# Two loads cut by partitions into 120 and 8: cosformer attention and a leaky-ReLU FFN on one core

## The chip, the core and the metric

The kernel runs on one core of a Trainium2 chip. The core has five engines with a queue of instructions each: TensorE (PE in the profile; its weight loads are PEld), VectorE (DVE), ScalarE (ACT), GpSimd (POOL) and SyncE (SP), which issues most of the transfers here. The transfers themselves are carried by 16 DMA engines. The metric is the device time of one execution in microseconds, lower is better.

## What is computed

Eight batches of linear attention with a cosine weighting, whose result (4608 tokens of 512 features) goes through a feed-forward layer with a leaky ReLU. All inputs and the output are float32.

```python
r = np.maximum(x, 0.0)
phi(x) = np.concatenate([r * cos_w, r * sin_w], axis=-1)
kv  = np.einsum('bhsf,bhsd->bhfd', k_p, v)          # k_p = phi(k), summed over the 576 tokens
z   = np.sum(k_p, axis=2)
num = np.einsum('bhsf,bhfd->bhsd', q_p, kv)          # q_p = phi(q)
den = np.einsum('bhsf,bhf->bhs', q_p, z)[..., None] + 1e-06
x   = (num / den), heads side by side -> (4608, 512)
h   = x @ w_in                                       # (512, 2048)
out = np.maximum(0.01 * h, h) @ w_out                # (2048, 512)
```

## The kernel before

Tokens are handled in nine groups of 512: the first 512 tokens of each batch, and a last group of all tails of 64. For each batch, q and k are turned into their two weighted halves (qp, kp) by DVE, ACT and POOL; TensorE sums kp against v into a small matrix per head (`kv_sum`, line 326); qp is transposed and multiplied with it (`num`, `num_half`); the quotient is transposed into xT, and the group goes through w_in (`ffn1` at line 486, later in a form with seven products of half blocks at line 638) and w_out (lines 512 and 755).

The start, in which the changed loads lie, is written out by hand. All its loads are issued by SP at once, in this order: q of batch 0 in two halves (`load_main`, line 121), then k and v of batch 0 in halves k, v, k, v (`load_kv`, line 135), then w_in in nine pieces (`load_w1`, line 167): block 0 as three pieces, blocks 1, 2 and 3 as two pieces each, where a block is 512 of the 2048 columns and a piece two of the four row chunks of 128. Behind them stand w_out (line 172), q, k and v of batch 1, and so on.

k and v lie with 128 partitions of 4 x 576 numbers; a half is 128 partitions of 2 x 576, 576 KB, two heads in each of two slots. A piece of two chunks of w_in is 128 partitions of 2 x 512, 512 KB.

The first half of k is read by DVE alone (`k_pair`, line 292, twice), which gives kp for `kv_sum(0, 0, 2)`. The second half is read by POOL and ACT (`k_cos`, line 253 on POOL and line 251 on ACT) and by DVE (`k_pair_half`), for `kv_sum(0, 2, 4)`. POOL then casts one quarter of v (`v_pairs`, line 261) and after that all nine pieces of w_in to float16 (`cast_w1`, line 261). Short runs of matmuls on a blank tile (`idle`, line 193) stand between TensorE's steps of the start.

Blocks 2 and 3 of w_in are staged in the constant tile ext, block 1 in wext, block 0 and the loads of q, k and v of batch 0 in the four buffers of the pool stage. TensorE takes the blocks in order: group 0 runs through columns of block 0, 1, 2, 3, and ACT's leaky ReLU (line 496) follows each pair of 128 columns.

Which engine does what, and where the later loads stand, is fixed by a table of positions; each load waits for its buffer.

Of the kernel before, what the change touches and what calls it, by code (L numbers as in the profile page):

```python
# [13 lines left out]
P = 128  # L14
# [6 lines left out]
def kernel(  # L21
# [14 lines left out]
    nc = tc.nc  # L36
# [41 lines left out]
    def psum(where, shape, dtype, name):  # L78
        p = {"h": ps_h, "o": ps_o, "n": ps_n}[where]
        return p.tile(shape, dtype, name=name, tag="ps_" + where)  # L80

    st = {}
# [21 lines left out]
    def stage_tile(nm, i, a, b, d):  # L104
        if (nm, i) in in_wext:
            return wext[:, 0 : a * b * d].rearrange("p (a b d) -> p a b d", a=a, b=b)
        if (nm, i) in in_ext:
            lo = NS * in_ext[nm, i]
            return ext[:, lo : lo + a * b * d].rearrange(
                "p (a b d) -> p a b d", a=a, b=b  # L110
            )
        return stage.tile([P, a, b, d], dt.float32, name=f"{nm}st", tag="stage")

    def load_main(nm, src, b, parts=(0, 1)):

        if parts[0] == 0:
            st[nm, b] = stage.tile([P, H, J, D], dt.float32, name=f"{nm}st", tag="stage")
        lo, hi = 4 * parts[0], 4 * parts[-1] + 4  # L120
        nc.sync.dma_start(
            st[nm, b][:, lo:hi],
            src[b, lo:hi, 0:MAIN, :].rearrange("h (p j) d -> p h j d", j=J),
        )

    def load_kv(nm, src, b, parts=(0, 1)):

        if parts[0] == 0:
            st[nm, b] = stage_tile(nm, b, NC, T, D)
        sl = slice(2 * parts[0], 2 * parts[-1] + 2)  # L130
        done.update((nm + "in", b, c) for c in range(sl.start, sl.stop))
        if parts[-1] == 1:
            done.add((nm + "in", b))
        rows = src[b].rearrange("h s d -> (h s d)").rearrange("(c p x) -> p c x", c=NC, p=P)
        nc.sync.dma_start(  # L135
            st[nm, b][:, sl].rearrange("p c j d -> p c (j d)"), rows[:, sl]
        )

    def load_qtail(i):
        t = stage.tile([P, H, D], dt.float32, name="qtl", tag="stage")  # L140
# [8 lines left out]
    w1 = {}  # L149
# [7 lines left out]
    w1v = moe_w_in.rearrange("(c p) f -> p c f", p=P)  # L157
# [4 lines left out]
    def load_w1(i, c, n):  # L162

        if c == 0:
            st["w1", i] = stage_tile("w1", i, 1, NKC, 512)[:, 0]
        sl = slice(c, c + n)
        nc.sync.dma_start(st["w1", i][:, sl], w1v[:, sl, 512 * i : 512 * (i + 1)])

    def load_w2(i, lo=0, hi=4):
        if lo == 0:  # L170
            st["w2", i] = stage_tile("w2", i, 1, 4, DM)[:, 0]
        nc.sync.dma_start(st["w2", i][:, lo:hi], w2v[i, :, lo:hi])

    load_main("q", q, 0, (0,))
    load_main("q", q, 0, (1,))
    for part in range(2):
        load_kv("k", k, 0, (part,))
        load_kv("v", v, 0, (part,))
# [3 lines left out]
    for part in w1_parts:  # L182
        load_w1(*part)
# [697 lines left out]
    ps = psum("h", [P, 2, 512], dt.float32, "ps_numh")  # L881
# [19 lines left out]
    for i in range(2):  # L901
        load_w2(i)
    load_main("q", q, 1)
    load_w2(2)
    load_kv("k", k, 1, (0,))
    load_w2(3, 0, 2)
    load_kv("v", v, 1, (0,))
# [55 lines left out]
    ps = psum("n", [P, 2, DM], dt.float32, "ps_o")  # L963
# [26 lines left out]
    ps = psum("h", [P, 2, MAIN], dt.float16, "ps_x")  # L990
# [239 lines left out]
```

## Time and profile before

| what | value |
|---|---|
| median of 3 runs | 274.8 us (274.21 to 275.55) |
| span of the profiled execution, first to last instruction | 272.6 us |
| own time of the profiled execution | not among the three times; the median lies 2.2 us above the span |
| TensorE matmul busy | 264.4 us, 97% |
| TensorE weight loads busy | 218.4 us, 80% |
| DVE, ACT, POOL busy | 205.4, 179.5, 128.9 us |
| moved by DMA | 57.07 MB, mean 209 GB/s |

Matmuls are pipelined and their ends are modelled, so a busy TensorE is not one at its peak. In the lines below, "L135" is line 135 of the kernel, "kp<-kst" names the tile written and the tile read, "x3" counts instructions merged in one row, and a bracket gives the idle time of the engine before the row and what ended it. SPq is SP's queue, which issues the transfers. The chain of waits is followed back from the last instruction: at each step to what released it, or to the instruction before it on its engine.

### The profile page before, as it was taken

How to read it: one execution, taken by the hardware profiler on the slowest of the kernel's cores; microseconds unless marked ns; L12 is line 12 of the kernel's file. 1: busy time of each engine (PE TensorE's matmuls, PEld its weight loads, DVE VectorE, ACT ScalarE, POOL GpSimd, SP SyncE). 2: the span in 40 equal slices, each digit the busy share in tenths (PEclk: the TensorE clock that was granted, in tenths of full speed). 3: DMA queues.
4: the chain of work that ended last, by engine and by line, in shares of the span. 5: the costliest groups of instructions: out<-in, count | busy, mean ns of one | idle time of the engine just before them, and what ended most of it. 6: DMA issues, size and time to landing. Idle time of an engine off the chain costs nothing.

```text
span 272.6 us, 7060 instructions
## 1 busy us (share of the span) xinstructions
PE 264.4 (97%) x2877; PEld 218.4 (80%) x2877; DVE 205.4 (75%) x419; ACT 179.5 (66%) x311; POOL 128.9 (47%) x104
## 2 busy tenths in 40 slices
PE   7899999999999999999999999999999999999993
PEld 2575454656975599999999999899999899999982
DVE  4940497788876796997989698897789957757852
ACT  7857447477976877898788786776744574565500
POOL 2676001992779366998893869733330004000000
PEclk9999999999999999999999999999999999999998
DMA  7999999999899899869979996884565052111214
GB/s 235 355 396 409 384 399 372 374 286 252 243 224 320 177 202 358 272 99 280 240 195 201 242 388 102 133 198 97 119 154 118 2 115 72 47 41 38 80 38 117
DMA packets 75040, 57.07 MB, mean 209 GB/s; under 512 B 47232, under 2 KB 63616, under 8 KB 74624
## 3 DMA queue, kind: packets, MB, share of 16 engines
q1 hardware_dynamic: 74400, 56.11, 74.2%
q10 hardware_dynamic: 608, 0.52, 0.6%
q8 instruction: 22, 0.36, 0.5%
q14 instruction: 10, 0.08, 0.1%
HBM read 36.70 MB, written 9.44 MB: 169 GB/s over the span
## 4 chain that ended last, share of the span: by engine, by line
PE 89%; DMA 3%; DVE 3%; POOL 1%; issue 1%; SPq 1%; ACT 1%; DVEq 0%
PE ps L755 33%; PE ps_f L638 26%; PE ps_h L486 15%; PE ps_o L512 5%; PE ps_kv L326 4%; DMA kst<-in_k_dram 3%; PE ps_num L412 3%; PE ps_f L755 1%; POOL kp L253 1%; PE ps_qt L398 1%; PE ps_xth L464 1%; PE ps_x L389 0%; DVE u L261 0%; ACT g L496 0%; SPq L135 0%
## 5 line engine op out<-in xcount | busy, mean ns | idle before, releaser
L755 PEld LDWEIGHTS <-g 128*128 128x128 f16 x640 | 61.8, 98 | 7.5 <-ACT g L496 0.6
L755 PE MATMUL ps<-w,g 128*128 128x256 f16 x496 | 65.3, 273 | 0.4 <-ACT g L496 0.4
L665 ACT ACTIVATE g<-ps_f 128x512 f16<-128x512 f32 x72 | 42.0, 599 | 19.9 <-PE ps_f L638 10.2
L486 PE MATMUL ps_h<-xT,w 128*128 128x512 f16 (+1 forms) x208 | 43.5, 363 | 0.1
L638 PEld LDWEIGHTS <-w 128*128 128x128 f16 x384 | 41.6, 114 | 1.1 <-issue 0.4
L638 PE MATMUL ps_f<-xT,w 128*128 128x256 f16 x288 | 42.1, 273 | 0.2 <-DVE u L261 0.2
L486 PEld LDWEIGHTS <-w 128*128 128x128 f16 x208 | 22.8, 114 | 16.3
L496 ACT ACTIVATE g<-ps_h 128x1024 f16<-128x1024 f32 x24 | 24.2, 1025 | 13.1 <-PE ps_h L486 13.1
L755 PE MATMUL ps<-T,ext 128*128 128x256 f16 x240 | 32.4, 273 | 0.0
L638 PEld LDWEIGHTS <-wext 128*128 128x128 f16 x288 | 31.2, 114 | 0.5
L253 POOL TENSOR_SCALAR kp<-kst,cos_t 128x256 f16<-128x256 f32 (+1 forms) x23 | 29.2, 1278 | 4.7 <-DMA kst<-in_k_dram 4.7
L755 PEld LDWEIGHTS <-ext 128*128 128x128 f16 x256 | 24.8, 98 | 2.5
L253 POOL TENSOR_SCALAR qp<-qst,cos_t 128x512 f16<-128x512 f32 (+1 forms) x10 | 19.5, 1947 | 9.2 <-DMA qst<-in_q_dram 7.7
L638 PE MATMUL ps_f<-X,wext 128*128 128x256 f16 x144 | 21.5, 273 | 0.0
L538 DVE TENSOR_TENSOR osb<-ps,ext 128x512 f32<-128x512 f32 x23 | 15.8, 689 | 7.4 <-PE ps L755 6.3
L253 POOL TENSOR_SCALAR kp<-kst,sin_t 128x256 f16<-128x256 f32 x15 | 19.0, 1269 | 4.0 <-PE ps_kv L326 2.7
L538 DVE TENSOR_TENSOR ps_f<-ps_f,u 128x512 f32<-128x512 f32 x24 | 16.7, 694 | 5.5 <-PE ps_f L638 3.2
L428 DVE TENSOR_TENSOR xs<-ps_num,rden 128x512 f16<-128x512 f32 x28 | 19.4, 691 | 1.0
L665 ACT ACTIVATE g<-y 128x512 f16<-128x512 f32 x24 | 15.2, 634 | 6.9 <-DVE y L538 6.6
L253 POOL TENSOR_SCALAR qp<-qst,sin_t 128x512 f16<-128x512 f32 (+1 forms) x10 | 19.6, 1963 | 0.0
L538 DVE TENSOR_TENSOR ext<-g 128x512 f16<-128x512 f16 (+1 forms) x24 | 14.1, 589 | 4.7 <-ACT g L496 3.0
L538 DVE TENSOR_TENSOR y<-ps_f,s 128x512 f32<-128x512 f32 x24 | 16.4, 685 | 1.4 <-PE ps_f L638 1.3
(120 smaller groups left out, 455.8 us busy)
## 6 DMA issues: line engine op xcount, KB each, us to landing
out_dram<-osb SPq DMA_DIRECT2D x32, 256.0 KB, 2.5
qst<-in_q_dram SPq DMA_DIRECT2D x7, 1024.0 KB, 9.1
kst<-in_k_dram SPq DMA_DIRECT2D x5, 1152.0 KB, 7.5
vst<-in_v_dram SPq DMA_DIRECT2D x5, 1152.0 KB, 9.8
w2st<-in_moe_w_out_dram SPq DMA_DIRECT2D x3, 1024.0 KB, 13.4
vst<-in_v_dram SPq DMA_DIRECT2D x4, 576.0 KB, 6.5
ext<-in_moe_w_in_dram SPq DMA_DIRECT2D x4, 512.0 KB, 11.0
kst<-in_k_dram SPq DMA_DIRECT2D x2, 576.0 KB, 7.4
```

What stands on the lines that cost most here:

```text
L253: eng.tensor_scalar(out=o, in0=i, scalar1=0.0, scalar2=col, op0=ALU.max, op1=ALU.mult)
L326: nc.tensor.matmul(ps[:, o, (c - lo) * NE : (c - lo + 1) * NE], lhsT=st["kp", b][sl, c, j, :], rhs=vm[sl, c, j, :], start=(j == 0), stop=( ...
L398: nc.tensor.transpose(ps[:, h, :], qp[:, h, :], ident)
L412: nc.tensor.matmul(ps[lo:hi, h // 4, (h % 4) * NE : (h % 4 + 1) * NE], lhsT=qpT[:, h, lo:hi], rhs=kv[b][:, h, :],)
L428: nc.vector.tensor_tensor(out=xs, in0=ps[:, :, 0 : 4 * NE].rearrange("p a (b e) -> p a b e", e=NE)[:, :, :, 0:D], in1=rden.rearrange("p (a ...
L486: nc.tensor.matmul(ps[:, m % 2, lo:hi], lhsT=w1[m // 4, c][0][:, w1[m // 4, c][1], m % 4 : 512 : 4], rhs=xT[:, lo // P : hi // P, c, :], s ...
L496: nc.scalar.activation(st["g", g][:, m - 1 : m + 1, :], ps, AF.Lrelu)
L512: nc.tensor.matmul(st["ps_o", g, tt], lhsT=st["g", g][:, m, tt * P : (tt + 1) * P], rhs=w2[:, m, :], start=(m == 0), stop=(m == NFT - 1),)
L538: eng.tensor_tensor(out=o, in0=a, in1=b, op=op)
L638: nc.tensor.matmul(ps[:, mi * HT : (mi + 1) * HT], lhsT=a[:, c, 2 * r0 + mi : 512 : 4], rhs=b[:, c], start=(n in (1, 5) and mi == 0 and c ...
L665: nc.scalar.activation(st["g", g][:, m : m + 2, r * HT : (r + 1) * HT], {"a": A, "c": y22, "e": E, "d": B_}[e].rearrange("p (m t) -> p m t ...
L755: nc.tensor.matmul(ps[:, tt], lhsT=a[:, i, tt * P : (tt + 1) * P], rhs=b[:, i], start=(first and i == 0), stop=(i == NPR - 1 and (apart or ...
```

## The change

A small function gives the ranges of partitions in which a load is issued: 0 to 120 and 120 to 128 for two named loads, all 128 for every other. Named are the first half of k of batch 0 and the first piece (chunks 0 and 1) of w_in's column block 2. For each of the two, SP issues two DMAs in place of one; what they write and read together is as before. The reading instructions wait for both.

```diff
+    apart = {("k", 0, 0), ("w1", 2, 0)}
+
+    def spread(key):
+
+        return (slice(0, 120), slice(120, P)) if key in apart else (slice(0, P),)
...
         rows = src[b].rearrange("h s d -> (h s d)").rearrange("(c p x) -> p c x", c=NC, p=P)
-        nc.sync.dma_start(
-            st[nm, b][:, sl].rearrange("p c j d -> p c (j d)"), rows[:, sl]
-        )
+        for ps in spread((nm, b, parts[0])):
+            nc.sync.dma_start(
+                st[nm, b][ps, sl].rearrange("p c j d -> p c (j d)"), rows[ps, sl]
+            )
...
         sl = slice(c, c + n)
-        nc.sync.dma_start(st["w1", i][:, sl], w1v[:, sl, 512 * i : 512 * (i + 1)])
+        for ps in spread(("w1", i, c)):
+            nc.sync.dma_start(
+                st["w1", i][ps, sl], w1v[ps, sl, 512 * i : 512 * (i + 1)]
+            )
```

## The prediction

> **What bounds the kernel now.** I read the page first: its span, the busy shares in slices, the queues and the chain of waits.
>
> ```profile
> span 272.6 us, 7060 instructions
> ...
> DMA  7999999999899899869979996884565052111214
> GB/s 235 355 396 409 384 399 372 374 286 252 243 224 320 177 202 358 272 99 280 240 195 201 242 388 102 133 198 97 119 154 118 2 115 72 47 41 38 80 38 117
> ...
> q8 instruction: 22, 0.36, 0.5%
> ...
> PE 89%; DMA 3%; DVE 3%; POOL 1%; issue 1%; SPq 1%; ACT 1%; DVEq 0%
> PE ps L755 33%; PE ps_f L638 26%; PE ps_h L486 15%; PE ps_o L512 5%; PE ps_kv L326 4%; DMA kst<-in_k_dram 3%; PE ps_num L412 3%; PE ps_f L755 1%; POOL kp L253 1%; PE ps_qt L398 1%; PE ps_xth L464 1%; PE ps_x L389 0%; DVE u L261 0%; ACT g L496 0%; SPq L135 0%
> ```
>
> TensorE carries 89% of the chain, and the one transfer in it is a load of k, 3%. A slice is 272.6/40 = 6.8 us; the DMA engines are nine tenths busy or more from the second slice to the tenth, at 355 to 409 GB/s, so in the first 60 us the queue of loads is never empty. Next I read the chain in order of time over the first 20 us, where both changed loads lie.
>
> ```profile
> 2.86 8.34 DMA kst<-in_k_dram
> ...
> 11.29 2.84 POOL kp L253 x3
> 14.12 0.62 POOL vm L261
> 14.79 0.75 PE ps_kv L326 x36
> ...
> 19.14 0.87 PE ps_h L486 x8
> ```
>
> The load that sets the pace is the one issued at 2.86 us and landed at 11.20: the second half of k, not the first half, which the change splits. POOL turns it into kp until 14.12, casts a quarter of v until 14.74, and TensorE sums k and v at 14.79. From 19.14 on TensorE runs on w_in. A microsecond won or lost at 11.20 reaches the end, because all behind it hangs on TensorE. Last I read who TensorE itself waits for in the whole run.
>
> ```profile
> PE ps_idle L193 <- DVE blank L188: 1.2, 1, 1.2
> PE ps_qt L398 <- DVE qp L253: 0.6, 1, 0.6
> PE ps_numh L448 <- ACT kv L333: 0.5, 1, 0.5
> PE ps_kv L326 <- POOL vm L261: 0.4, 1, 0.4
> PE ps L755 <- ACT g L496: 0.4, 1, 0.4
> PE ps_xth L464 <- DVE xs L428: 0.2, 1, 0.2
> PE ps_x L389 <- ACT xT L259: 0.2, 1, 0.2
> PE ps_f L638 <- DVE u L261: 0.2, 1, 0.2
> PE ps_qt L398 <- POOL qp L253: 0.2, 1, 0.2
> ```
>
> No transfer stands there. Matmul ends are modelled, so these waits are lower bounds, but the chain, which goes by what released each step, names no transfer after k either.
>
> **The change part by part.** It takes away two DMAs of 128 partitions and puts four in their place: 120 and 8 partitions of k's first half, and 120 and 8 of the first piece of w_in's column block 2. Bytes, packets per row and every compute instruction stay. The rows for the cost of a load:
>
> ```profile
> 1.79 0.51 SPq L135 DMA_DIRECT2D kst<-in_k_dram  x1
> 2.34 0.47 SPq L135 DMA_DIRECT2D vst<-in_v_dram  x1
> 2.86 0.57 SPq L135 DMA_DIRECT2D kst<-in_k_dram  x1
> ...
> 8.21 0.76 DVE L292 SCALAR_TENSOR_TENSOR kp<-kst,cos_t 128x576 f16<-128x576 f32 x1 [0.52 <-DMA kst<-in_k_dram]
> ...
> 9.72 1.25 ACT L259 CAST vm<-vst 128x576 f16<-128x576 f32 x2 [0.28 <-DMA vst<-in_v_dram]
> ...
> 11.03 0.74 PE L326 MATMUL ps_kv<-vm,kp 64*128 64x66 f16 x36
> 11.29 2.84 POOL L253 TENSOR_SCALAR kp<-kst,cos_t 128x128 f16<-128x128 f32 x3 [2.60 <-DMA kst<-in_k_dram]
> ...
> 13.87 0.66 ACT L259 CAST vm<-vst 128x576 f16<-128x576 f32 x1
> ...
> 14.05 0.39 PE L464 MATMUL ps_xth<-ident,xs 128*128 128x128 f16 x4
> ...
> 14.79 0.75 PE L326 MATMUL ps_kv<-vm,kp 64*128 64x66 f16 x36 [0.35 <-POOL vm L261]
> ```
>
> *Issue.* SP spends 0.47 to 0.57 us on a DMA and goes on to the next, so the extra issue puts v's first half, k's second half and all behind them some 0.5 us later into the queue. k's second half would be issued at about 3.4 instead of 2.86 us and its data start only when the v load before it is through, about 9.7; 6 us of queue cover it. Cost 0; without that cover, 0.5 us.
>
> *Moving the bytes of k.* Three loads of 576 KB land in a row and each is waited for: 8.21, 9.72, 11.29, so 1.5 us each. Over 16 engines, 8 of the 128 rows an engine, a row is 1.5/8 = 0.19 us of one engine. What the trace of before does not show is how 120 and 8 rows are dealt out. From below: dealt evenly, the sum is the same and the cost is 0. If 15 engines take 8 rows each and then 8 engines take one more, those 8 are 0.19 us later and the sixteenth is 1.5 us ahead. From above: 120 rows on 8 engines are 15 rows in place of 8, 7 x 0.19 = 1.3 us, with the eight rows behind them 1.5; or the 8 rows all on one engine, 8 x 0.19 = 1.5. A gain can't be excluded either: a load lands with its slowest engine, and the spared one may be that. Its size has a cap: ACT's cast of the other quarter of v ends at 13.87 + 0.66 = 14.53, against 14.74 for POOL's, so TensorE's sum cannot start more than 0.2 us earlier. I take +0.1 us, the middle of the even deal (0) and the one-row deal (0.19), which keep nearest to the 8 rows an engine of these rows; the ends, -0.2 and +1.5, go into the range.
>
> The Trainium skill, DMA: Bandwidth & Descriptors, section "Why a DMA increments its semaphore by 16 and not by 1", says that a DMA runs on the largest number of engines up to 16 that divides its slowest dimension, the lowest-numbered ones: 120 rows on 15, 8 rows on 8. No run here shows it yet; by it the term is between 0 and +0.19, and one engine is spared. The same page, "Rules for kernel authors", speaks against cutting a load by partitions: two such transfers share the same engines and serialize, so nothing would be won; the 1.5 us steps between loads of these rows agree that loads queue behind each other.
>
> *The waits of the first half.* The DVE work on the first half now waits for two landings. If they come 0.2 us late, kp and the first sum of k and v (11.03) are 0.2 us late, and so all that follows to TensorE's transposes at 14.05, which end at 14.44. The next sum starts at 14.79 for POOL's sake, so 0.35 us is hidden. Behind DVE's waiting instruction stand only the later kp steps, of that same chain. Cost 0; beyond 0.35 us each further microsecond counts in full.
>
> *The piece of w_in and the queue behind it.*
>
> ```profile
> 6.02 2.55 SPq L167 DMA_DIRECT2D wext<-in_moe_w_in_dram  x2
> ...
> 9.71 4.33 SPq L167 DMA_DIRECT2D ext<-in_moe_w_in_dram  x4
> ...
> 14.43 2.78 SPq L172 DMA_DIRECT2D w2st<-in_moe_w_out_dram  x2
> ...
> 20.82 1.04 POOL L261 CAST w<-ext 128x1024 f16<-128x1024 f32 x1 [0.31 <-DMA ext<-in_moe_w_in_dram]
> 22.18 1.04 POOL L261 CAST w<-ext 128x1024 f16<-128x1024 f32 x1 [0.31 <-DMA ext<-in_moe_w_in_dram]
> ...
> 26.10 1.02 ACT L496 ACTIVATE g<-ps_h 128x1024 f16<-128x1024 f32 x1 [0.65 <-PE ps_h L486]
> ...
> 27.80 1.23 DVE L261 CAST w<-w2st 128x2048 f16<-128x2048 f32 x1 [9.18 <-DMA w2st<-in_moe_w_out_dram]
> 27.83 1.02 ACT L496 ACTIVATE g<-ps_h 128x1024 f16<-128x1024 f32 x1 [0.70 <-PE ps_h L486]
> ```
>
> A 512 KB piece takes 22.18 - 20.82 = 1.36 us, a row 0.17. Both splits together put an engine at most 0.36 us behind in the one-row deal. Block 2 is cast by 22.18 + 1.04 = 23.22. TensorE needs it for the group whose activation starts at 26.10; groups follow at 27.83 - 26.10 = 1.73 us, so that one starts near 24.37. That covers 1.15 us: cost 0, and beyond 1.15 us one for one.
>
> In the built order each SP issue from the ninth DMA on waits for the landing of the eighth before it (eight semaphores are dealt out in turn). One more DMA moves every such wait to a later partner: the first load at line 167 into wext, issued at 6.02 now, waits for the 120 rows of k, about 8.2; w_out's first load moves from 14.43 by about one w_in piece, 1.4 us. At 8.2 there are v, k and v (3 x 1.5) and block 0 of w_in (two pieces' worth, 2 x 1.36) still to move, 7 us; at 15.8 five pieces of w_in, 7 us. The engines do not run dry. Cost 0; without this cover, up to 2 us. Past those few issues every wait again names the DMA it named before, and stores and transposes keep their places on SP, so later stages move only with the shift of TensorE.
>
> **Sum.** 0 (issue) + 0.1 (k's landing) + 0 (first half) + 0 (w_in) + 0 (semaphores) = +0.1 us on 272.6: 272.7. The profiled execution's own time is not among those shown; the median of the three runs, 274.8, is 2.2 above the span, which I add: 274.9.
>
> **Rivals.** *The pieces run on few engines (slower).* 120 rows on 8 engines, or 8 rows on one, put k's second half 1.5 us later: the chain passes 11.29, so 276.4. For it: nothing in the trace shows a load of such a shape, and each of the 16 engines has its 8 rows now. Against it: 120 has divisors other than 8. It decides as soon as k lands over 0.35 us late on DVE, or at all on POOL.
>
> *The spared engine was the late one (a little faster).* The instruction queue's 22 packets take 0.5% of 16 engines' span, 0.005 x 16 x 272.6/22 = 1 us each, on one engine at a time, and a load lands with its last engine. If that engine, or one late from the start, is the spared one, loads land up to 1 us earlier from then on. But at 11.20 the cap is 0.2 us, and w_in has 1.15 us in hand: 274.6.
>
> *Earlier landings shorten the later stages (faster).* The chain gives 3% to DVE, about 8 us, mostly after the start. If a microsecond on every load up to 60 us moved DVE and POOL forward in it, 1.5 us might go: 273.3. Against it: no transfer releases a step of the chain after 11.20, so these waits are on DVE's own order.
>
> **How the numbers follow.** Forecast 0.56; few engines 0.19; spared engine 0.13; later stages 0.12. About 0.5%, 1.4 us here, is what a measurement can tell from no change. The forecast (274.9) and the spared engine (274.6) lie within it: same 0.69. Few engines is +1.6, slower 0.19; later stages is -1.5, faster 0.12. The bounds of k's term alone give 274.6 to 276.3; the three runs shown scatter by 0.6 below and 0.75 above their median. The range 273.4 to 276.4 takes in both outer cases only at their edges; it leaves out about 2 in 10.
>
> **What would show it.** Right: SP issues k's first half twice, some 0.5 us apart; DVE's first kp starts at 8.2 to 8.4; POOL's first kp between 11.2 and 11.5; TensorE's second sum between 14.6 and 15.0; POOL's casts of w_in still about 1.36 us apart; no transfer in the chain after k. Few engines: POOL's kp near 12.8. Spared engine: casts of w_in earlier by a microsecond, with the end unmoved. Wrong: TensorE waiting for a transfer after 19 us, a DMA share that falls in the first 60 us, or a chain whose DVE share changes by a microsecond or more.

## The result and the profile after

The changed kernel takes 276.35 us (median of 8 runs, 275.52 to 276.55), the kernel before 274.83 us (8 runs): a ratio of 1.0052, with the interval 1.0038 to 1.0065. It is 1.5 us slower, at the upper edge of the range that was given, where 274.9 was forecast. The profiled execution took 275.93 us, with a span of 274.1.

The page of the changed kernel: its span, the DMA share and the rate in 40 slices, and the chain by engine.

```profile
span 274.1 us, 7063 instructions
...
DMA  7999999999999899789989997786565051110214
GB/s 214 338 335 353 390 398 375 382 349 240 284 179 283 253 183 345 246 160 252 242 221 195 224 396 128 117 207 102 117 141 130 2 115 51 68 41 25 93 38 116
...
PE 89%; DMA 3%; DVE 2%; POOL 1%; issue 1%; SPq 1%; ACT 1%; DVEq 0%
```

The span is 1.5 us longer, and the chain of waits by engine has the same shares within a point. The digits of the DMA share are as before in the first ten slices: the engines are counted as just as busy. What they moved is not: the second slice has 338 in place of 355 GB/s, the third 335 in place of 396, the fourth 353 in place of 409. So the cut loads do not leave engines idle; the engines take longer for the same bytes. The packets say the same one by one: from 18 to 22 us, while the cut piece of w_in moves, the median packet of 2048 B takes 144 ns, where it took 88 before. The same is plainer in stretches of 4 us, before and after; the last two columns are the DMA share and GB/s.

```profile
5.00:9.00 4.00, 3.22 (x33) 2.04 (x32) 3.48 (x12) 3.18 (x6) 2.50 (x2) 1.00 1.03 368
9.00:13.00 4.00, 3.53 (x72) 2.37 (x70) 4.00 (x7) 3.72 (x9) 1.71 (x2) 1.00 0.99 331
18.00:22.00 4.00, 4.00 (x35) 3.38 (x33) 0.62 (x1) 2.69 (x4) 3.12 (x3) 1.00 1.05 386
```

```profile
5.00:9.00 4.00, 2.92 (x31) 1.86 (x30) 2.71 (x10) 3.14 (x6) 2.46 (x2) 1.00 1.02 243
9.00:13.00 4.00, 3.00 (x54) 1.80 (x51) 3.24 (x5) 2.56 (x4) 0.54 (x1) 1.00 1.04 388
18.00:22.00 4.00, 3.75 (x44) 3.53 (x43) 2.01 (x6) 1.19 (x3) 1.44 (x3) 1.00 1.07 239
```

While the cut half of k moves, 5 to 9 us, 243 GB/s in place of 368; while the cut piece of w_in moves, 18 to 22 us, 239 in place of 386; between them, with whole loads alone, 388. The first stretch is short of 4 x (368 - 243) = 500 KB, which is 1.36 us at 368 GB/s. The second is short of 590 KB, 1.5 us.

The chain of the changed kernel in order of time, and then the instructions that answer to those shown of before (in the timeline; a bracket is the idle time before).

```profile
3.17 9.21 DMA kst<-in_k_dram
...
12.46 3.19 POOL kp L263 x3
15.65 0.62 POOL vm L271
...
16.32 0.75 PE ps_kv L336 x36
```

```profile
1.79 0.89 SPq L142 DMA_DIRECT2D kst<-in_k_dram  x2
...
3.17 0.47 SPq L142 DMA_DIRECT2D kst<-in_k_dram  x1
...
9.76 0.76 DVE L302 SCALAR_TENSOR_TENSOR kp<-kst,cos_t 128x576 f16<-128x576 f32 x1 [2.04 <-DMA kst<-in_k_dram]
...
10.90 1.25 ACT L269 CAST vm<-vst 128x576 f16<-128x576 f32 x2 [1.44 <-DMA vst<-in_v_dram]
...
12.46 3.19 POOL L263 TENSOR_SCALAR kp<-kst,cos_t 128x128 f16<-128x128 f32 x3 [3.75 <-DMA kst<-in_k_dram]
...
16.32 0.75 PE L336 MATMUL ps_kv<-vm,kp 64*128 64x66 f16 x36 [0.36 <-POOL vm L271]
...
24.02 2.15 POOL L271 CAST w<-ext 128x1024 f16<-128x1024 f32 x2 [1.01 <-DMA ext<-in_moe_w_in_dram]
...
27.75 1.02 ACT L506 ACTIVATE g<-ps_h 128x1024 f16<-128x1024 f32 x1 [0.77 <-PE ps_h L496]
```

The path is the one read before the change: k's second half, POOL's kp, POOL's quarter of v, the second sum. Each link is later: k's first half on DVE 8.21 to 9.76, v's first half on ACT 9.72 to 10.90, POOL's kp 11.29 to 12.46 (+1.17), and the second sum 14.79 to 16.32 (+1.53), the rest being POOL's three kp, 2.84 to 3.19 us. The activation g at 26.10, the first of the single ones, moves to 27.75. From it to the end are 272.6 - 26.10 = 246.5 us before and 274.1 - 27.75 = 246.35 after, so the whole loss is made by then.

How the two pieces were dealt out can be counted in the trace's landings: they are reported one by one. The 120 rows show 15 of them, from 7.79 to 9.24 us, and the 8 rows show 8, from 8.32 to 9.66. DVE goes at 9.76, behind the last of them. By the Trainium skill, DMA: Bandwidth & Descriptors, section "Why a DMA increments its semaphore by 16 and not by 1", 120 rows run on 15 engines and 8 rows on 8; the trace agrees with its 15 and 8 landings. So neither deal that the rival of few engines needs took place (120 rows on 8 engines, or 8 rows on one), and yet the loads are late.

### The profile page after: what moved, and what is told of

Its sections match the earlier page's. It is cut to its first block, busy times and chain, and to the rows that moved or that the text cites. A ratio compares the mean times of both kernels' runs of the same rounds, so it can differ in the third digit from the quotient of the medians.

```text
span 274.1 us, 7063 instructions
## 1 busy us (share of the span) xinstructions
PE 264.7 (97%) x2877; PEld 218.4 (80%) x2877; DVE 205.1 (75%) x419; ACT 179.3 (65%) x311; POOL 131.3 (48%) x104
## 4 chain that ended last, share of the span: by engine, by line
PE 89%; DMA 3%; DVE 2%; POOL 1%; issue 1%; SPq 1%; ACT 1%; DVEq 0%
PE ps L765 33%; PE ps_f L648 26%; PE ps_h L496 15%; PE ps_o L522 5%; PE ps_kv L336 4%; DMA kst<-in_k_dram 3%; PE ps_num L422 3%; PE ps_f L765 1%; POOL kp L263 1%; PE ps_qt L408 1%; PE ps_xth L474 1%; SPq L142 0%; PE ps_x L399 0%; ACT g L506 0%; SPq L127 0%
## 5 line engine op out<-in xcount | busy, mean ns | idle before, releaser
L263 POOL TENSOR_SCALAR kp<-kst,cos_t 128x256 f16<-128x256 f32 (+1 forms) x23 | 31.7, 1386 | 5.7 <-DMA kst<-in_k_dram 3.7
```

The lines of the kernel that those rows point to most:

```text
L263: eng.tensor_scalar(out=o, in0=i, scalar1=0.0, scalar2=col, op0=ALU.max, op1=ALU.mult)
```

## The experiments

Three theories were set against each other. A: rows of a load that is not whole are dealt so that several engines write into the same part of SBUF at a time and share its rate, so that each packet takes longer. B: the loss comes from the numbers of engines, 15 and 8 in place of 16. C: the second DMA in itself costs. The first four were timed beside 31 runs of the kernel before (median 274.90 us), e5 to e8 beside 19 on another chip (274.84), e10 beside 17 on a third (274.57); each ratio goes by its own group. The table has the starts read from one profiled execution of each kernel, and the median of all its runs, in us:

| kernel | what is cut | DVE's first kp | POOL's kp | second sum | g | median | ratio and interval |
|---|---|---|---|---|---|---|---|
| before | nothing | 8.21 | 11.29 | 14.79 | 26.10 | 274.83 | |
| changed | k first half, w_in piece, 120 and 8 | 9.76 | 12.46 | 16.32 | 27.75 | 276.35 | 1.0052 (1.0038 to 1.0065) |
| e1 | k alone, 120 and 8 | 10.46 | 13.24 | 17.02 | 28.32 | 275.97 | 1.0039 (1.0018 to 1.0061) |
| e2 | w_in alone, 120 and 8 | 8.39 | 11.47 | 14.97 | 26.67 | 275.34 | 1.0014 (0.9994 to 1.0034) |
| e3 | k, 64 and 64 | 9.06 | 11.84 | 15.62 | 26.93 | 275.00 | 0.9999 (0.9981 to 1.0017) |
| e4 | k, 112 and 16 | 9.57 | 12.18 | 16.13 | 27.44 | 275.40 | 1.0015 (0.9993 to 1.0037) |
| e5 | k by slot, 128 and 128 | 7.50 | 10.78 | 14.84 | 26.15 | 274.66 | 0.9996 (0.9978 to 1.0013) |
| e6 | nothing; k, k, v, v | 8.24 | 9.76 | 15.84 | 27.15 | 275.66 | 1.0047 (1.0025 to 1.0070) |
| e7 | both halves of k, 120 and 8 | 9.66 | 14.94 | 18.86 | 30.17 | 279.01 | 1.0159 (1.0137 to 1.0182) |
| e8 | v second half, 120 and 8 | 8.22 | 12.44 | 16.35 | 27.66 | 276.14 | 1.0054 (1.0039 to 1.0068) |
| e10 | k, even and odd rows | 7.93 | 11.30 | 15.21 | 26.53 | 274.36 | 0.9985 (0.9965 to 1.0006) |

Two of the medians carry a lower granted clock beside the change: it was 0.991 to 0.994 in all four runs of e7 and 0.99 in three of e6's eight, where most other runs have 0.996 or more. The starts in the table are the firmer reading for these two.

### One cut at a time (e1, e2)

```diff
-    apart = {("k", 0, 0), ("w1", 2, 0)}
+    apart = {("k", 0, 0)}        # e1
+    apart = {("w1", 2, 0)}       # e2
```

> Only the first half of k is loaded as 120 and 8 partitions; w_in's piece is whole again. All theories that put the loss at the start (k's second half landing at 12.37 instead of 11.20 us, TensorE's second sum at 16.32 instead of 14.79) expect nearly the whole loss to stay: +1.3 to +1.5 us on the time before. The rival, that w_in's piece shares in the loss because TensorE waited 0.4 us for POOL's cast near 26 us, expects +0.9 to +1.1. In both, DVE's first kp starts near 9.8 us.

> Only the first piece of w_in's column block 2 is loaded as 120 and 8 partitions; k's half is whole. If the start carries the loss: DVE's first kp back at 8.2 us, TensorE's second sum at 14.8, POOL's casts of block 2 about 1.2 us late (near 22 and 23.4 instead of 20.82 and 22.18), and the time +0 to +0.2 us, since 1.15 us of cover stand before TensorE needs the block. If w_in's piece shares in the loss: +0.4 us or more.

The timeline of e1, and then that of e2 with what its TensorE did at block 2.

```profile
13.24 3.11 POOL L263 TENSOR_SCALAR kp<-kst,cos_t 128x128 f16<-128x128 f32 x3 [4.44 <-DMA kst<-in_k_dram]
...
17.02 0.75 PE L336 MATMUL ps_kv<-vm,kp 64*128 64x66 f16 x36 [0.37 <-POOL vm L271]
```

```profile
14.97 0.75 PE L336 MATMUL ps_kv<-vm,kp 64*128 64x66 f16 x36 [0.37 <-POOL vm L271]
...
22.95 2.14 POOL L271 CAST w<-ext 128x1024 f16<-128x1024 f32 x2 [1.02 <-DMA ext<-in_moe_w_in_dram]
...
25.15 2.13 PE L496 MATMUL ps_h<-xT,w 128*128 128x512 f16 x9 [0.19 <-POOL w L271]
...
26.67 1.02 ACT L506 ACTIVATE g<-ps_h 128x1024 f16<-128x1024 f32 x1 [1.03 <-PE ps_h L496]
```

k alone gives 1.0039, whose interval holds the whole change's 1.0052; w_in alone gives 1.0014, which is not told apart from 1. By their medians, though, both came out where the rival put them: e1 +1.07 us (275.97 - 274.90) and e2 +0.44 (275.34 - 274.90), which add up to the 1.5 of the whole change. The intervals are too wide to decide, so the times leave open how much w_in's piece adds. In e1's profiled run k is even later than in the changed kernel (13.24 against 12.46); that execution took 276.67 us against its median of 275.97, the changed kernel's 275.93 against 276.35, so one execution places the landing of this cut no better than to some 0.7 us, and smaller differences in the table's starts prove little by themselves. In e2 block 2 is cast by 22.95 + 2.14 = 25.09 where it was 23.22: 1.87 us late. TensorE waits for it (0.19), and g is 0.57 late, of which 0.18 was there at the second sum. In the changed kernel TensorE is itself 1.53 late by then, and g adds only 1.65 - 1.53 = 0.12: in that execution k's delay covers most of w_in's.

### Other ways to cut k (e3, e4, e5)

```diff
-        return (slice(0, 120), slice(120, P)) if key in apart else (slice(0, P),)
+        return (slice(0, 64), slice(64, P)) if key in apart else (slice(0, P),)      # e3
+        return (slice(0, 112), slice(112, P)) if key in apart else (slice(0, P),)    # e4
...
+        one = (nm, b, parts[0]) == ("k", 0, 0)                                      # e5
+        for cs in (slice(0, 1), slice(1, 2)) if one else (sl,):
+            nc.sync.dma_start(
+                st[nm, b][:, cs].rearrange("p c j d -> p c (j d)"), rows[:, cs]
+            )
```

e3 and e4 cut k alone. 64, 112 and 16 rows can all be dealt to 16 engines, so that B expects nothing of them; the trace shows 16 landings for each of these loads. e5 also makes two DMAs of one, but each has all 128 partitions and one of the two slots.

> Only k's first half is cut, into 64 and 64 partitions, rows that divide evenly over 16 engines. Theory A (a load of fewer than 128 partitions is dealt so that several engines write one part of SBUF at a time, and every packet is slower): DVE's first kp starts 1 to 1.6 us later than 8.2 us, time +1 to +1.6 us. Theory B (the loss is the number of engines, 15 and 8, or a row count that is no power of two): kp at 8.2 to 8.4 us, time 0 to +0.2 us. Theory C (the second DMA and the second landing themselves cost): kp about 9.6 us, time +1 to +1.5 us, as with any cut.

> Only k's first half is cut, into 112 and 16 partitions: 7 rows and 1 row on each of 16 engines. Theory A (which part of SBUF each engine writes): DVE's first kp 1 us or more later than 8.2 us, time +0.8 to +1.5 us. Theory B (fewer than 16 engines): kp at 8.2 to 8.4 us, time 0 to +0.2 us. Theory C (any second DMA): +1 to +1.5 us.

> k's first half is loaded by two DMAs of all 128 partitions, one for each of its two slots, so there is a second DMA, a second landing and the same shift of the semaphores, but no cut by partitions. Theory A (partitions): DVE's first kp at 8.2 to 8.6 us, TensorE's second sum within 0.3 us of 14.79, time within 0.3 us of before. Theory C (any second DMA): kp 9.0 us or later and time +0.5 us or more.

The stretch from 5 to 9 us in e3, in e4, and then in e5 with its POOL and its second sum.

```profile
5.00:9.00 4.00, 2.53 (x28) 1.61 (x26) 2.45 (x9) 3.40 (x6) 2.64 (x2) 1.00 1.02 264
```

```profile
5.00:9.00 4.00, 3.62 (x33) 2.14 (x32) 2.70 (x10) 3.16 (x6) 2.51 (x2) 1.00 1.01 267
```

```profile
5.00:9.00 4.00, 3.59 (x28) 1.99 (x26) 4.00 (x11) 3.15 (x6) 2.89 (x2) 1.00 1.03 366
```

```profile
10.78 2.83 POOL L255 TENSOR_SCALAR kp<-kst,cos_t 128x128 f16<-128x128 f32 x3 [1.62 <-DMA kst<-in_k_dram]
...
14.84 0.74 PE L328 MATMUL ps_kv<-vm,kp 64*128 64x66 f16 x36
```

64 and 64 rows move 264 GB/s, and k lands 0.55 us late (11.84); 112 and 16 move 267 GB/s, with k 0.89 late (12.18). Their times alone do not show a loss (both intervals hold 1), and by their medians they lost less than A expected (+0.1 and +0.5 us); DVE's first kp, 0.85 and 1.36 us late, is under A's range in e3 and within it in e4. It is the rate, down by over a quarter, that shows the loss. Two DMAs of 128 partitions move 366, like the 368 of one, and the second sum stays within 0.05 us: C falls, and B is not what slows the loads of e3 and e4. e5 also fits the cap of the prediction: POOL starts 0.5 us earlier than before and is done with its quarter of v at 14.24, but ACT casts the other quarter only from 14.33 to 14.99, and the sum is not earlier. ACT is itself late there because the first sum is (11.51 in place of 11.03), behind a wait of TensorE for POOL's qp (0.63 us) and not for a load.

### Whether k's second half alone sets the pace (e6)

Nothing is cut; both halves of k are issued before both halves of v.

```diff
     for part in range(2):
         load_kv("k", k, 0, (part,))
+    for part in range(2):
         load_kv("v", v, 0, (part,))
```

> Nothing is cut; SP issues both halves of k before both halves of v. If POOL's kp for the second sum, which waits for k's second half, is what sets the start: that half lands near 9.7 us, POOL is done with kp near 12.6, TensorE's second sum moves from 14.8 to 13.5 to 14.2, time -0.5 to -1.2 us. Rival: the first sum, which needs v's first half, is pushed from 11.0 to 12.5 us and takes the place of the wait removed: second sum at 14.8 or later, time 0 to +0.5 us.

```profile
9.76 3.85 POOL L254 TENSOR_SCALAR kp<-kst,cos_t 128x128 f16<-128x128 f32 x3 [1.05 <-DMA kst<-in_k_dram]
11.23 1.25 ACT L260 CAST vm<-vst 128x576 f16<-128x576 f32 x2 [1.75 <-DMA vst<-in_v_dram]
11.96 1.03 PE L327 MATMUL ps_kv<-vm,kp 64*128 64x66 f16 x36 [0.84 <-ACT vm L260]
...
15.84 0.74 PE L327 MATMUL ps_kv<-vm,kp 64*128 64x66 f16 x36
```

POOL's kp starts 1.53 us earlier than before, and yet the kernel is slower: by 0.47% at the median, by some 0.6 us in the five runs at the higher clock (275.43 to 275.79). That is a little beyond what the rival expected. v's first half is now late on ACT (11.23), the first sum with it (11.03 to 11.96), and the second at 15.84. So k's second half does not set the pace alone: v's first half has little to spare, and takes its place when it is late.

### A second cut, and a cut behind the load that sets the pace (e7, e8)

```diff
-    apart = {("k", 0, 0), ("w1", 2, 0)}
+    apart = {("k", 0, 0), ("k", 0, 1)}    # e7
+    apart = {("v", 0, 1)}                 # e8
```

> Both halves of batch 0's k are cut into 120 and 8 partitions, w_in is whole. Theory A with a price per cut: k's second half lands about twice as late as in the changed kernel, at 13.2 to 13.9 us instead of 12.37, TensorE's second sum at 17.0 to 17.9, time +2 to +3 us. Rival, that the price is paid once, by the first load that follows q: second sum near 16.3 and time +1.2 to +1.6 us.

> Only the second half of batch 0's v is cut into 120 and 8 partitions. It lands near 12.6 us before and is first read at 13.9 by ACT and 14.1 by POOL. Theory A with cover: it lands at 13.5 to 14.3, k is unmoved (kp at 8.2, POOL's kp at 11.3), TensorE's second sum moves by 0 to 0.3 us, and the time by 0 to +0.3 us. Rival, that a cut costs the whole queue behind it and so the end: +0.8 us or more.

The timeline of e7, then that of e8 and its stretch from 9 to 13 us.

```profile
14.94 3.25 POOL L263 TENSOR_SCALAR kp<-kst,cos_t 128x128 f16<-128x128 f32 x3 [6.21 <-DMA kst<-in_k_dram]
...
18.86 0.75 PE L336 MATMUL ps_kv<-vm,kp 64*128 64x66 f16 x36 [0.85 <-POOL vm L271]
```

```profile
2.85 0.47 SPq L142 DMA_DIRECT2D kst<-in_k_dram  x1
3.36 0.91 SPq L142 DMA_DIRECT2D vst<-in_v_dram  x2
...
12.44 3.25 POOL L263 TENSOR_SCALAR kp<-kst,cos_t 128x128 f16<-128x128 f32 x3 [3.73 <-DMA kst<-in_k_dram]
...
16.35 0.75 PE L336 MATMUL ps_kv<-vm,kp 64*128 64x66 f16 x36 [1.06 <-POOL vm L271]
```

```profile
9.00:13.00 4.00, 3.53 (x72) 2.37 (x70) 3.21 (x5) 3.62 (x8) 0.56 (x1) 1.00 1.04 269
```

With both halves cut POOL's kp is 3.65 us late and the second sum 4.07, nearly twice what e1 gave (1.95 and 2.23), so a second cut is paid for again; the price is beyond the range that was expected (second sum at 17.0 to 17.9). e8 is the surprise: it was expected to leave k unmoved and to cost 0.3 us at most, and it cost 1.3. k's second half is whole, and issued at 2.85 as before, ahead of the cut load of v (3.36). Yet it lands 1.15 us late (POOL 11.29 to 12.44), and the rate of that stretch falls from 331 to 269 GB/s. A cut load slows the whole load ahead of it: the first of its 16 landings comes when it did before (10.10 us, 10.12 before), the last at 12.35 in place of 11.20. That the engines which are through with their share of k go on into v and disturb the ones still at k fits this, and is argued, not shown.

### Where the rows lie (e10, e9)

e10 cuts k into two pieces of 64 rows like e3, but takes the even and the odd partitions.

```diff
-        return (slice(0, 120), slice(120, P)) if key in apart else (slice(0, P),)
+        return (slice(0, P, 2), slice(1, P, 2)) if key in apart else (slice(0, P),)
```

> Only k's first half is cut, into its even and its odd partitions, 64 rows each, so two DMAs of 64 partitions as in the cut into 64 and 64, but each spread over all 128 partitions. Theory A (which part of SBUF the rows lie in, not that there are 64 of them): packets of the cut load nearer to 93 ns than in the cut into lower and upper half, DVE's first kp at 8.2 to 8.7 us instead of 9.06, TensorE's second sum at 14.7 to 15.2 instead of 15.62, time within 0.3 us of before. If any cut by partitions pays: kp near 9.1, second sum near 15.6.

```profile
5.00:9.00 4.00, 3.62 (x33) 2.21 (x32) 3.70 (x11) 3.22 (x6) 2.49 (x2) 1.00 1.01 341
```

The same numbers of rows and of DMAs as e3, and 341 GB/s in place of 264, DVE's first kp at 7.93 and POOL's at 11.30, close to 8.21 and 11.29 before; the median packet of 2304 B in that stretch takes 93 ns, as before, against 138 in e3. So it is not the count of rows that costs, but which rows. The second sum comes at 15.21, 0.42 later than before, because POOL's three kp take 3.25 us there; the time shows no loss.

e9 measures the loads by themselves: the kernel before, and behind its last store some loads of k's rows in packets of 2304 B, into buffers that nothing reads. Its time, 405.74 us in a single run, says nothing of the change.

```diff
+    def probe(name, ps, n, parts=1):
+        for r in range(n):
+            t = stage.tile([P, NC, T * D], dt.float32, name=name, tag="stage")
+            for c in range(0, NC, NC // parts):
+                cs = slice(c, c + NC // parts)
+                nc.sync.dma_start(t[ps, cs], src[ps, cs])
...
+    probe("pwhole", slice(0, P), 4, 2)
+    probe("pcut", slice(0, 120), 4, 2)
+    probe("pmid", slice(0, P), 4, 2)
+    probe("phalf", slice(0, 64), 8, 2)
+    probe("phalfstep", slice(0, P, 2), 8, 2)
+    probe("peight", slice(120, P), 16)
+    probe("peightstep", slice(96, P, 4), 16)
+    probe("pend", slice(0, P), 4, 2)
```

> The kernel before, and behind its last store loads of batch 0's k into idle buffers, back to back, one shape after the other with nothing else running: 8 loads each of 128, 120 and again 128 partitions (2 x 576 numbers a partition), 16 each of the first 64 and of every second of 128 partitions, 16 each of 8 neighbouring partitions (120 to 127) and of 8 that stand 4 apart (96, 100 to 124) with 4 x 576 numbers; then 128 again. The time of the whole says nothing; the packets of 2304 bytes, 93 ns each in whole loads at the start of the kernel before, do. Theory A (several engines write one part of SBUF at a time): 120 partitions 140 to 190 ns a packet, 64 neighbouring ones 170 ns or more, 8 neighbouring ones 180 ns or more, 8 that stand 4 apart near 93 ns, 128 near 93 ns throughout. Theory B (fewer engines, or rows that don't divide by 16): 120 slower, 64 near 93 ns, and both sets of 8 alike. Rival that it is the mixture with other loads and not the shape: all near 93 ns.

One stretch inside each group of loads, in the order of the diff; the last two columns are the DMA share and GB/s.

```profile
276.00:282.00 6.00, 0.50 1.04 400
287.00:301.00 14.00, 0.50 1.03 257
306.00:313.00 7.00, 0.50 1.05 381
318.00:334.00 16.00, 0.50 1.03 203
340.00:349.00 9.00, 0.50 0.81 257
362.00:372.00 10.00, 0.50 0.53 54
378.00:386.00 8.00, 0.50 0.34 98
393.00:400.00 7.00, 0.50 1.03 395
```

Whole loads move 400, 381 and 395 GB/s. 120 rows move 257 and the first 64 rows 203, with the DMA share at 1.03 in both: the engines are counted as fully busy and each packet takes longer. In the three other groups the rate says less. Eight rows show 8 landings a load, so half of the engines take part: the share of 0.53 for the neighbouring ones is that half, busy all the time. Every second row and eight rows four apart (0.81 and 0.34) leave engines idle between SP's issues. So the packets tell it, in the trace's record of each:

```
rows                      median ns of a 2304 B packet
128 (three groups)         93, 95, 93
0 to 119                  142
0 to 63                   184
0, 2, 4 ... 126            93
120 to 127                352
96, 100 ... 124            93
```

Sixty-four neighbouring rows take 184 / 93 = 2.0 times as long a packet, eight neighbouring ones 3.8 times; the same numbers spread over the partitions take no longer than a whole load. A holds for what it says of place: neighbouring rows get in each other's way. Rows that are neighbours in SBUF are neighbours in HBM too in these loads of k (2304 B apart), and no run here parts the two. Against HBM as the cause speaks w_in's cut piece: its rows stand 8192 B apart in HBM, nearly as far as those of k that are taken four apart (9216 B, 93 ns), and yet its packets slow from 88 to 144 ns. By the Trainium skill, SBUF — State Buffer, section "Door 1: The DMA port swizzle (why `[64,N]` ≈ `[32,N]`)", SBUF is reached through 16 ports, and rows 0 to 63 lie on 8 of them, rows 120 to 127 on two, the spread ones on more: two engines a port for the 64, four for the eight, which agrees with 2.0 and 3.8. Which engine takes which of the 120 rows no run here shows, so their 142 / 93 = 1.5 is measured and not derived.

## Why the prediction was wrong about the size

The measured time lies 0.05 us inside the upper end of the range, and that is luck: this end was put there for few engines, which did not happen, and a loss of this size was given a chance of 0.19.

*What bounds the kernel* held: the path from k's second half over POOL to the second sum is the chain of the changed kernel too, and what was lost at 16.32 was still lost at the end.

*Issue, 0.* Right. SP issued k's second half 0.3 us later (2.86 to 3.17), and in e5, with the same extra DMA, both halves of k and the first half of v were read earlier than before (DVE 7.50, POOL 10.78, ACT 9.33).

*Moving the bytes of k, +0.1: the step that failed.* It measured +1.17 at POOL's kp and, with POOL's three kp 0.35 us longer, +1.53 at the second sum. The step counted rows an engine and priced a row at 0.19 us, taken from whole loads. The landings, 15 and 8, fit its own one-row deal, which gives +0.19 at most, but the price of a row is not fixed: a packet takes 93 ns in a whole load and 142 in one of 120 rows (e9). The bound of +1.5 fits only in size, as it had been worked out from few engines.

*The waits of the first half, 0.* The 0.35 us of cover were gone: DVE's first kp is 1.55 late. It added nothing to the sum, since the second sum is still released by POOL's vm (0.36), late for the same reason. The changed kernel's TensorE waited for both halves of its first sum, as the list of its waits shows:

```profile
PE ps_kv L336 <- DVE kp L302: 0.5, 1, 0.5
PE ps_kv L336 <- ACT vm L269: 0.5, 1, 0.5
```

*The piece of w_in, 0.* The same wrong price: the step put an engine at most 0.36 us behind, and e2 measured 1.87 at the cast of block 2. The cover of 1.15 was about right, since 1.87 - 1.15 = 0.7 against the 0.57 that g moved in e2. In the changed kernel k's delay took it in, and w_in is left with 0.12 in the profiled execution. The step on the semaphores of eight held: the first load into wext was issued at 9.26, right behind the last landing of the 120 rows (9.24, later than the 8.2 that was expected), and the DMA share stays at 1.02 or above in the three stretches shown, so the engines do not run dry.

*The rivals.* Few engines gave 276.4, the measured time almost to the tenth, with the right place and the wrong cause. It put POOL's kp near 12.8, where 12.46 was read, and it needed 8 engines for 120 rows or one for 8, but the landings say 15 and 8. The point from which it decides was right: k's lateness counts as soon as it reaches POOL. The spared engine was not the late one, and no cast came earlier. Later stages gave nothing: from g to the end 246.5 us became 246.35.

*What would show it.* Of the signs for being right, DVE's first kp (8.2 to 8.4) was at 9.76, POOL's (11.2 to 11.5) at 12.46, the second sum (14.6 to 15.0) at 16.32; and the casts of block 2 follow one another without the old step of 1.36 (two in 2.15 us from 24.02). Two signs came true: SP issues k's first half twice, 0.6 us apart (1.79 and 2.39), and the chain names no transfer after k. Of the signs for being wrong, TensorE's wait for a transfer and a falling DMA share did not come. The share was the wrong column; the one beside it, GB/s, fell by a third. The third sign came by the letter: the chain's share on DVE falls from 3% to 2%. In the chain of the kernel before, these two steps stood in the middle stage and are gone after:

```profile
166.01 0.69 DVE s L261
166.71 0.60 DVE u L261
```

That 1.3 us of the chain now goes another way and wins nothing, by the 246 us from g to the end.

## What to carry to other kernels

A load that reaches all 128 partitions is not the sum of loads that reach some of them: cut along the free dimension (e5), or into even and odd partitions (e10), and the time shows no loss; cut into runs of neighbouring partitions, and each packet takes about 1.5 to 4 times as long (142 to 352 ns in place of 93 in e9). Read GB/s beside the DMA share, because in these runs the engines counted as busy while they moved a third less. And price the neighbours: in these runs the load ahead of the cut one (e8) and the ones behind it (e1) were late too.

## What the runs showed of the hardware that was not expected

A load of 120 partitions moved 257 GB/s where one of 128 moved 400, with a DMA share of 1.03 against 1.04. Eight neighbouring rows took 352 ns a packet of 2304 B, eight rows four apart took 93. A cut load delayed the whole load issued before it by 1.15 us (e8, one execution).

One of POOL's three kp is longer than the others, and by how much differs between kernels: 1.45 us against 0.71 before the change, 1.81 after, 1.86 in e10. The three take 2.84 us before, 3.19 after, 3.25 in e10 at the same start as before (11.30), and 3.85 in e6. DVE works on kp during these in all of them; whether the overlap is what costs was not tried, and stays open. No cut beats the kernel before beyond its interval: e10 (0.9985) and e5 (0.9996) both hold 1.
